# Strassen's seven products for the first layer of a second network, with its factors and input kept in a DRAM scratch

## The chip, the cores and the metric

The kernel runs on one NeuronCore of a Trainium2 chip. TensorE multiplies, VectorE (DVE), ScalarE (ACT) and GpSimd (POOL) do the elementwise work, SyncE (SP) issues every DMA. The metric is the device time of one execution in microseconds: the median of several runs.

## The reference

Three stages follow each other, all in float32:

```python
# attention, 4 batches x 8 heads x 576 positions x 64: local mask (4 heads), strided mask (4 heads)
scores = scale * q @ k.T, masked;  attn = softmax(scores);  x = attn @ v        # 2304 tokens x 512
# first network: maximum of three gates
h = np.maximum(np.maximum(x @ w1, x @ w2), x @ w3)                              # 512 -> 768
x = h @ w_out                                                                   # 768 -> 512
# second network: a leaky rectifier with a slope for each hidden unit
h = x @ w_in                                                                    # 512 -> 2048
g = np.maximum(h, 0.0) + alpha * np.minimum(h, 0.0)
out = g @ w_out                                                                 # 2048 -> 512
```

## The kernel before

Everything sits with features on the 128 partitions and tokens along the free axis. The networks' products are made in three passes: each operand is kept as two float32r words, `hi` (rounded by ScalarE) and `lo = a - hi` (subtracted by VectorE or GpSimd), and a product is hi*hi + hi*lo + lo*hi, three matmuls (`PAIRS`, L348). The helper `split` (L94) makes the two words, so all these operations carry the lines L96 and L99.

The weights arrive as 64-bit floats. `from_double` (L101) makes float32 of a block of 128 x 512: one ScalarE instruction (L112), two on VectorE (L115, L117), then the split (ScalarE, GpSimd). A `Converter` moves blocks through this line, one step per unit of TensorE's work.

The program is one order written out by hand. First come the four batches b = 0 to 3, each of 576 tokens. In a batch, 36 gate units (`gate_unit`, L354; 12 matmuls of 288 columns each) and 8 output units (`out1_unit`, L372; 18 matmuls each) of the first network are issued in turn. Between them stand the steps of the next batch's attention, and in batch 0 those of the weights' conversion. Batch 3 converts the second network's 32 blocks, and goes on with that in the first block of the second network. The result of the first network is copied from PSUM into x2 tiles that stay in SBUF (L380).

Then comes the second network over six blocks of 384 tokens. For each of 16 chunks f of 128 hidden units, `h_unit` (L493) issues 12 matmuls of 384 columns into one of three PSUM banks; VectorE applies the rectifier from PSUM (L502, L504), the split follows, and two chunks later `o_unit` (L512) adds the chunk into three output banks: 3 matmuls of 512 columns for each of 3 token tiles. After the 16th chunk each output bank is copied by ScalarE (L523) and stored (L524). All DMAs wait in SyncE's queue in program order.

Of the kernel before, what the change touches and what calls it, by code (L numbers as in the profile page):

```python
# [17 lines left out]
DM = 512  # L18
F1 = 768
F2 = 2048  # L20
P = 128
# [9 lines left out]
BLK = 384  # L31
NBLK = NT // BLK
BIG = -8.0e9
# [12 lines left out]
STARTS_LAST = tuple(range(1, NUNITS, 2))  # L46
LO_ON_POOL = (0, B - 1)
# [3 lines left out]
def attention_maxout_prelu_kernel(  # L51
# [49 lines left out]
    def from_double(raw, floats, dst, fetch):  # L101
# [19 lines left out]
        t = dst()  # L121
        split(t[:, 0], t[:, 1], a.bitcast(F32), nc.scalar, nc.gpsimd)
# [3 lines left out]
    hx, xx, x0x, ax, h0x, psx, stage_x = (ExitStack() for _ in range(7))  # L126
# [4 lines left out]
    wp = pool(ctx, "wp", 24)  # L131
    hp = pool(hx, "hp", 8)
    tp = pool(xx, "tp", 3)
# [187 lines left out]
    class Converter:  # L321


        def __init__(self, blocks, raws, floats):
            self.blocks, self.raws, self.floats = list(blocks), raws, floats
            self.sources = [src for src, _, _ in self.blocks]
            self.fetched, self.line = [], []
# [8 lines left out]
        def step(self):  # L336

            if self.blocks:
                _, key, weights = self.blocks.pop(0)

                def dst():
                    words[key] = weights().tile([P, 2, DM], F32R, tag="w", name="w")
                    return words[key]

                self.line.append(from_double(self.fetched.pop(0), self.floats, dst, self.fetch))
            self.line = [block for block in self.line if next(block, False)]
# [4 lines left out]
    x2 = {}  # L351
# [20 lines left out]
    def out1_unit(b, hf, dc, st):  # L372
        acc = bank()[:, :HALF]
        n = 0
        for f in range(NF1):
            for wi, xi in PAIRS:
# [3 lines left out]
        nc.scalar.copy(x2[b][:, dc, hf * HALF:(hf + 1) * HALF], acc)  # L380
# [5 lines left out]
    GATES = [(0, 0), (0, 1), (0, 2), (1, 0), (0, 3), (0, 4), (1, 1), (0, 5), None,  # L386
             (1, 2), (1, 3), (1, 4), (1, 5), None]
    GATES_LAST = [(hf, f) for f in range(NF1) for hf in range(2)] + [None, None]

    def first_net(b, gates, lo_engine, more):  # L390
        st = {}
        hf_out = 0
        for n, what in enumerate(gates):
# [5 lines left out]
            else:  # L399
                for g in range(3):  # L400
                    gate_unit(b, *what, g, st, lo_engine, hp if n < 8 else more)
                    yield


    x2h = {}

    def split_x2(x2p, blk):
        for cc in range(NCC):
            t = x2p.tile([P, 2, BLK], F32R, tag=f"x2h{cc}", name=f"x2h{cc}")
            done = 0  # L410
# [10 lines left out]
    blocks = [(w1[f, g], ("gate", f, g), lambda: wp) for f in range(NF1) for g in range(3)]  # L421
    blocks += [(wo1[f], ("mix", f), lambda: wp) for f in range(NF1)]
# [89 lines left out]
    def o_unit(blk, f, t):  # L512
# [6 lines left out]
        if f < NF2 - 1:  # L519
            return  # L520
# [87 lines left out]
```

## Time and profile before

| what | value |
|---|---|
| median of 3 runs | 815.6 us (815.19 to 816.21) |
| profiled execution, own time | 818.03 us |
| its span in the trace | 816.3 us |
| first network, batch 0 to batch 3 | to about 413 us of the span |
| second network | 413.0 to 812.6 us of the span |

The profile is read from the busy shares of the engines to the stretch in question, from there to the durations of single instructions, and last to the moments at which two engines want the same thing. A row of a group by line gives busy time, mean duration of one instruction and the idle time of the engine just ahead of it. A row of the timeline gives start, length and number of the instructions that were merged.

### The profile page before, as it was taken

Reading aid. Unit: us, or ns where it says so; the run is one execution under the profiler, and the core shown is the slowest. Engines: PE = TensorE matmul, PEld = TensorE weight load, DVE = VectorE, ACT = ScalarE, POOL = GpSimd, SP = SyncE. Lnnn points to the kernel's source line nnn. Section 1 sums busy time; section 2 is a strip of 40 time slices with the busy share of each in tenths; the row PEclk is TensorE's granted clock in tenths of the full one; section 3 lists DMA queues with packets and bytes.
Section 4 is the critical chain, followed back from the end, with each engine's and each line's share of the span. In section 5 each row is a group of like instructions: output and inputs, shape, how many; then the busy total and the mean of one; then the engine's idle time right before and its main releaser. Section 6 shows DMA issues by size and latency. Waiting matters only on the chain.

```text
span 816.3 us, 13289 instructions
## 1 busy us (share of the span) xinstructions
PE 789.7 (97%) x5200; PEld 735.2 (90%) x5200; DVE 378.5 (46%) x1006; ACT 281.0 (34%) x845; POOL 170.7 (21%) x176
## 2 busy tenths in 40 slices
PE   6688899999999999999999999999999999999998
PEld 5578799999999999999999999999999999999997
DVE  5669671243314423165657254454444445445442
ACT  7646683254324443255454121121111112112111
POOL 4456661022101111066458310000000000000000
PEclk9789899999999999999999999999999999999999
DMA  7437521020111100255444010001001001001001
GB/s 254 142 104 244 191 94 56 8 61 21 49 62 32 50 21 1 104 155 159 152 132 128 0 39 1 1 1 39 1 1 39 1 0 40 1 1 39 0 1 39
DMA packets 17775, 50.28 MB, mean 62 GB/s; under 512 B 2096, under 2 KB 2096, under 8 KB 17712
## 3 DMA queue, kind: packets, MB, share of 16 engines
q1 hardware_dynamic: 17712, 49.43, 18.6%
q8 instruction: 41, 0.67, 0.3%
q14 instruction: 22, 0.18, 0.1%
HBM read 44.70 MB, written 4.72 MB: 61 GB/s over the span
## 4 chain that ended last, share of the span: by engine, by line
PE 92%; ACT 3%; DMA 2%; DVE 2%; issue 1%; POOL 0%; SPq 0%; POOLq 0%; ACTq 0%; DVEq 0%
PE bank L359 27%; PE ph L498 25%; PE po L517 24%; PE bank L377 10%; PE bank L191 3%; PE bank L252 2%; PE bank L235 2%; ACT e L209 1%; DMA k<-in_kTs 1%; DMA raw<-in_w 1%; DVE word L115 1%; ACT word L112 0%; ACT w L96 0%; POOL e L223 0%; DVE e L203 0%
## 5 line engine op out<-in xcount | busy, mean ns | idle before, releaser
L359 PE MATMUL bank<-x,w 128*128 128x288 f32 x1728 | 247.3, 300 | 2.2 <-POOL w L99 2.2
L359 PEld LDWEIGHTS bank<-x,w 128*128 128x128 f32 x1728 | 232.6, 190 | 8.0 <-POOL w L99 2.4
L498 PE MATMUL ph<-x2h,w 128*128 128x384 f32 x1152 | 218.0, 339 | 0.0
L498 PEld LDWEIGHTS ph<-x2h,w 128*128 128x128 f32 x1152 | 205.4, 188 | 6.8
L517 PE MATMUL po<-w,g 128*128 128x512 f32 x864 | 210.2, 389 | 0.0
L517 PEld LDWEIGHTS po<-w,g 128*128 128x128 f32 x864 | 161.0, 188 | 26.7
L96 ACT CAST g<-neg 128x384 fp32r<-128x384 f32 x96 | 49.4, 514 | 315.8 <-DVE neg L504 315.8
L502 DVE TENSOR_SCALAR neg<-ph,alpha_sb 128x384 f32<-128x384 f32 x96 | 59.2, 617 | 155.1 <-PE ph L498 149.6
L366 DVE TENSOR_TENSOR t<-bank,t 128x288 f32<-128x288 f32 x96 | 43.7, 455 | 124.4 <-PE bank L359 111.8
L223 POOL TENSOR_TENSOR e<-e,rc 96x384 f32<-96x384 f32 (+2 forms) x64 | 49.1, 788 | 189.8 <-DVE rc L221 182.3
L99 POOL TENSOR_TENSOR w<-word,w 128x512 fp32r<-128x512 f32 x56 | 75.6, 1358 | 26.5 <-ACT w L96 24.2
L377 PE MATMUL bank<-h,w 128*128 128x288 f32 x576 | 80.3, 297 | 0.0
L209 ACT ACTIVATE e<-e,nm 96x128 f32<-96x128 f32 (+2 forms) x176 | 67.5, 386 | 32.6 <-DVE nm L203 32.6
L377 PEld LDWEIGHTS bank<-h,w 128*128 128x128 f32 x576 | 77.0, 188 | 1.3
L99 DVE TENSOR_TENSOR g<-neg,g 128x384 fp32r<-128x384 f32 x80 | 44.7, 559 | 52.4 <-ACT g L96 52.4
L117 DVE SCALAR_TENSOR_TENSOR word<-raw,word 128x512 uint32<-128x512 uint32 x56 | 54.8, 979 | 1.9
L504 DVE SCALAR_TENSOR_TENSOR neg<-ph,neg 128x384 f32<-128x384 f32 x96 | 53.5, 558 | 3.3
L96 ACT CAST h<-t 128x288 fp32r<-128x288 f32 x48 | 20.7, 432 | 83.8 <-DVE t L366 83.6
L115 DVE TENSOR_SCALAR word<-word 128x512 uint32<-128x512 uint32 x56 | 37.9, 677 | 8.4 <-ACT word L112 8.3
L191 PE MATMUL bank<-k,q 64*96 64x128 f32 (+2 forms) x352 | 30.0, 308 | 11.1 <-DMA k<-in_kTs 11.1
L112 ACT ACTIVATE word<-raw 128x512 f32<-128x512 f32 x56 | 37.5, 670 | 4.7 <-DMA raw<-in_w 4.3
L99 POOL TENSOR_TENSOR h<-t,h 128x288 fp32r<-128x288 f32 x24 | 25.8, 1076 | 62.0 <-ACT h L96 62.0
(39 smaller groups left out, 400.8 us busy)
## 6 DMA issues: line engine op xcount, KB each, us to landing
raw<-in_w SPq DMA_DIRECT2D x50, 512.0 KB, 3.6
q<-in_qT SPq DMA_DIRECT2D x16, 288.0 KB, 3.4
out_dram<-osb SPq DMA_DIRECT2D x18, 256.0 KB, 2.2
v<-in_vl SPq DMA_DIRECT2D x8, 384.0 KB, 3.0
raw<-in_wo SPq DMA_DIRECT2D x6, 512.0 KB, 3.6
v<-in_vs SPq DMA_DIRECT2D x8, 320.0 KB, 4.1
k<-in_kTl SPq DMA_DIRECT2D x8, 304.0 KB, 3.8
k<-in_kTs SPq DMA_DIRECT2D x8, 288.0 KB, 4.0
```

What stands on the lines that cost most here:

```text
L96: hi_engine.copy(hi, src)
L99: lo_engine.tensor_tensor(out=lo, in0=src, in1=hi.bitcast(F32), op=ALU.subtract)
L117: nc.vector.scalar_tensor_tensor(out=a, in0=low, scalar=29, in1=a, op0=ALU.logical_shift_right, op1=ALU.bitwise_or)
L191: nc.tensor.matmul(sc[j][:nq, KT * i:KT * i + nk], q[rows, qo:qo + nq], k[rows, ko:ko + nk], start=True, stop=True)
L209: nc.scalar.activation(e[:nq, j, i, :nk], e[:nq, j, i, :nk], AF.Exp, bias=nm[:nq, j, i:i + 1], scale=-1.0, accum_out=sm[:nq, j, i:i + 1])
L223: nc.gpsimd.tensor_tensor(out=e[:nq, j, :n, :nk], in0=e[:nq, j, :n, :nk], in1=rc[:nq, j, :n].unsqueeze(2).to_broadcast([nq, n, nk]), op=AL ...
L359: nc.tensor.matmul(acc, words["gate", f, g][:, wi, cc * P:(cc + 1) * P], xt[b, cc, hf][:, xi, :], start=n == 0, stop=n == 3 * NCC - 1)
L377: nc.tensor.matmul(acc, words["mix", f][:, wi, dc * P:(dc + 1) * P], st["h", hf, f][:, xi, :], start=n == 0, stop=n == 3 * NF1 - 1)
L498: nc.tensor.matmul(acc, words[0, f][:, wi, cc * P:(cc + 1) * P], x2h[blk, cc][:, xi, :], start=n == 0, stop=n == 3 * NCC - 1)
L502: nc.vector.tensor_scalar(out=neg, in0=acc, scalar1=0.0, scalar2=alpha_sb[:, f:f + 1], op0=ALU.min, op1=ALU.mult)
L504: nc.vector.scalar_tensor_tensor(out=neg, in0=acc, scalar=0.0, in1=neg, op0=ALU.max, op1=ALU.add)
L517: nc.tensor.matmul(acc, g[:, gi, t * P:(t + 1) * P], words[1, f][:, wi], start=f == 0 and i == 0, stop=f == NF2 - 1 and i == 2)
```

## The change

The second network now works on three blocks of 768 tokens, and on pairs of hidden chunks (`n` counts 24 groups: 8 pairs q for each of 3 blocks). The first layer of a pair is a 2 x 2 block product: two halves of the contraction, two chunks, two halves of 384 tokens. It is made with seven products in place of eight, of 6 matmuls each (2 contraction chunks x 3 passes), in two PSUM banks a and b_ that alternate (`h_products`). The sums of weights that this needs (`odd_chunk`) are made in batches 1 and 2, split, and stored to a DRAM scratch `hd`; in each group the four factors of the group after next are loaded from there (`load_pair`). The sums of x (`load_x2`) are made by GpSimd from the first network's result, which goes to DRAM in `out1_unit` and comes back. VectorE adds the products (`add`) and applies the rectifier from SBUF (`hidden`). The output products of group n (12 units of 3 matmuls, `o_units`) are issued between the products of group n+1.

Of the 16 second-layer chunks, 12 are converted in batch 3, and 4 in batch 2 by way of DRAM. In batch 3 the lo words of the first network are made by VectorE instead of GpSimd.

```diff
-BLK = 384
+BLK = 768
+HB = BLK // 2
+NQ = NF2 // 2
...
-LO_ON_POOL = (0, B - 1)
+DIRECT = 12
+CONVERT = tuple(15 * j // 4 for j in range(2 * NF2 - DIRECT))
+LOAD_X, SPLIT_X = 20, 35
...
+    def store(a, place):
+        t = wst.tile([P, 2, DM], F32R, tag="w", name="w")
+        n = a.shape[1]
+        nc.scalar.copy(t[:, 0, :n], a)
+        yield True
+        nc.vector.tensor_tensor(out=t[:, 1, :n], in0=a, in1=t[:, 0, :n].bitcast(F32), op=ALU.subtract)
+        yield True
+        nc.sync.dma_start(place[:, :, :n], t[:, :, :n].bitcast(F32))
...
+    def odd_chunk(q):
...
+            for out_, x, y, op in ((c[:, :half], e[:, :half], a[:, :half], ALU.subtract),
+                                   (a[:, :half], a[:, :half], a[:, half:], ALU.add),
+                                   (c[:, half:], a[:, :half], e[:, :half], ALU.subtract),
+                                   (d[:, :half], e[:, half:], c[:, half:], ALU.subtract)):
+                nc.vector.tensor_tensor(out=out_, in0=x, in1=y, op=op)
+            yield True
+            for x, place in ((a, hd[q][1]), (c, hd[q][2]), (d[:, :half], hd[q][3])):
+                yield from store(x, place)
...
     def out1_unit(b, hf, dc, st):
-        nc.scalar.copy(x2[b][:, dc, hf * HALF:(hf + 1) * HALF], acc)
+        xo = tp.tile([P, HALF], F32, tag="t", name="xo")
+        nc.scalar.copy(xo, acc)
...
+            nc.sync.dma_start(x2d[i][:, dc, s:s + nn], xo[:, done:done + nn])
...
+    def load_x2(blk):
+        for i in range(2):
+            t = xsp.tile([P, 2, 2, HB], F32, tag="xs", name="xs")
+            for h in range(2):
+                nc.sync.dma_start(t[:, :, h, :], x2d[2 * blk + h][:, i::2, :])
...
+            for out_, x, y in ((t3, b22, b12), (b12, b12, b11), (t2, b22, b12), (t4, b21, t2)):
+                nc.gpsimd.tensor_tensor(out=out_, in0=x, in1=y, op=ALU.subtract)
...
+    def split_x2(blk, k):
+        name = PRODUCTS[k][1]
+        for i in range(2):
...
+            split(t[:, 0], t[:, 1], xs.pop((blk, name, i)), nc.scalar, nc.gpsimd if blk else nc.vector)
...
-    gp = pool(ctx, "gp", 3)
-    ps_h = ctx.enter_context(tc.tile_pool(name="ps_h", bufs=3, space=PSUM, reuse_waits="tile"))
-    ps_o = ctx.enter_context(tc.tile_pool(name="ps_o", bufs=5, space=PSUM, reuse_waits="tile"))
+    gp = pool(ctx, "gp", 8)
+    cp = pool(ctx, "cp", 8)
+    osp = pool(ctx, "osp", 2)
+    ps_h = ctx.enter_context(tc.tile_pool(name="ps_h", bufs=2, space=PSUM, reuse_waits="tile"))
+    ps_o = ctx.enter_context(tc.tile_pool(name="ps_o", bufs=6, space=PSUM, reuse_waits="tile"))
...
+    def hidden(n, j, half, h):
+        f = 2 * (n % NQ) + j
+        neg = cp.tile([P, HB], F32, tag="c", name="neg")
+        nc.vector.tensor_scalar(out=neg, in0=h, scalar1=0.0, scalar2=alpha_sb[:, f:f + 1], op0=ALU.min, op1=ALU.mult)
+        nc.vector.scalar_tensor_tensor(out=neg, in0=h, scalar=0.0, in1=neg, op0=ALU.max, op1=ALU.add)
+        g = gts[n, j, half] = gp.tile([P, 2, HB], F32R, tag="g", name="g")
+        late.append(lambda: nc.scalar.copy(g[:, 0], neg))
+        if (j, half) != (0, 1):
+            late.pop()()
+        late.append(lambda: nc.vector.tensor_tensor(out=g[:, 1], in0=neg, in1=g[:, 0].bitcast(F32), op=ALU.subtract))
...
+        product(0, a)
+        u = temp()
+        nc.scalar.copy(u, a)
+        rest()
+        yield
+        product(1, b_)
+        v = temp()
+        add(v, b_, u)
+        yield
+        product(2, a)
+        add(u, a, u)
+        hidden(n, 0, 0, u)
+        yield
+        product(3, b_)
+        w = temp()
+        add(w, b_, v)
+        rest()
+        yield
+        product(4, a)
+        x = temp()
+        add(x, a, w)
+        add(v, a, v)
+        hidden(n, 1, 1, x)
+        yield
+        product(5, b_)
+        add(w, b_, w)
+        rest()
+        hidden(n, 1, 0, w)
+        yield
+        product(6, a)
+        add(v, a, v)
+        rest()
+        hidden(n, 0, 1, v)
+        yield
...
+    for n in range(NQ * NBLK):
+        blk, q = divmod(n, NQ)
+        if n + 2 < NQ * NBLK:
+            load_pair(n + 2)
+        if q == 4 and blk + 1 < NBLK:
+            load_x2(blk + 1)
+        for i, _ in enumerate(h_products(n)):
+            if n == 0 and EARLY_X + 1 + i < 7:
+                split_x2(0, EARLY_X + 1 + i)
+            elif q == NQ - 1 and blk + 1 < NBLK and i > 1:
+                split_x2(blk + 1, i - 2)
+            elif q == 0 and blk and i < 2:
+                split_x2(blk, 5 + i)
+            for _ in range((i + 1) * 12 // 7 - i * 12 // 7):
+                next(outs, None)
+        outs = o_units(n)
```

On TensorE, in the middle of the second network, this stood in a row before. A row is one line's matmuls: PSUM bank, x words, weight words, shape and count.

```order
L498 MATMUL ph_7568<-x2h0_7519,w_4344 128x384 x3
L498 MATMUL ph_7568<-x2h1_7522,w_4344 128x384 x3
L498 MATMUL ph_7568<-x2h2_7525,w_4344 128x384 x3
L498 MATMUL ph_7568<-x2h3_7528,w_4344 128x384 x3
L517 MATMUL po_7152<-w_5444,g_7516 128x512 x3
L517 MATMUL po_7156<-w_5444,g_7516 128x512 x3
L517 MATMUL po_7160<-w_5444,g_7516 128x512 x3
```

Now, from the sixth product of one group to the second of the next (x50 is the first half of the sixth product's x words, `ph_8060` bank a of one group, `ph_8184` the same bank in the next):

```order
L660 MATMUL ph_8061<-x50_7664,w_7800 128x384 x3
L660 MATMUL ph_8061<-x51_7667,w_7800 128x384 x3
L619 MATMUL po_7903<-w_4928,g_8007 128x512 x3
L619 MATMUL po_7882<-w_4890,g_8045 128x512 x3
L660 MATMUL ph_8060<-x60_7681,w_7804 128x384 x3
L660 MATMUL ph_8060<-x61_7684,w_7804 128x384 x3
L619 MATMUL po_7886<-w_4890,g_8045 128x512 x3
L619 MATMUL po_7903<-w_4890,g_8045 128x512 x3
L660 MATMUL ph_8184<-x00_7539,w_7928 128x384 x3
L660 MATMUL ph_8184<-x01_7542,w_7928 128x384 x3
L619 MATMUL po_7818<-w_4969,g_8099 128x512 x3
```

Twelve matmuls into one of three banks, then nine of the output, became six into one of two banks, then one or two output units of three.

On VectorE, where the second network begins, this stood before (word is a weight block under conversion, neg the rectified chunk):

```order
L117 SCALAR_TENSOR_TENSOR word_5030<-raw_4918,word_5030 128x512
L502 TENSOR_SCALAR neg_5110<-ph_5097,alpha_sb_64 128x384
L504 SCALAR_TENSOR_TENSOR neg_5110<-ph_5097,neg_5110 128x384
L115 TENSOR_SCALAR word_5079<-word_5079 128x512
L117 SCALAR_TENSOR_TENSOR word_5079<-raw_4979,word_5079 128x512
L502 TENSOR_SCALAR neg_5138<-ph_5125,alpha_sb_64 128x384
```

Now, from the last x words of the first block on (`ph_5552` is bank a, `ph_5553` bank b_, c the temporaries):

```order
L104 TENSOR_TENSOR x51_5565<-t_5028,x51_5565 128x384
L665 TENSOR_TENSOR c_5574<-ph_5553,c_5560 128x384
L104 TENSOR_TENSOR x60_5576<-xs_5013,x60_5576 128x384
L104 TENSOR_TENSOR x61_5579<-xs_5023,x61_5579 128x384
L665 TENSOR_TENSOR c_5560<-ph_5552,c_5560 128x384
L639 TENSOR_SCALAR neg_5589<-c_5560,alpha_sb_64 128x384
L641 SCALAR_TENSOR_TENSOR neg_5589<-c_5560,neg_5589 128x384
L665 TENSOR_TENSOR c_5600<-ph_5553,c_5574 128x384
L647 TENSOR_TENSOR g_5592<-neg_5589,g_5592 128x384
L665 TENSOR_TENSOR c_5609<-ph_5552,c_5600 128x384
L665 TENSOR_TENSOR c_5574<-ph_5552,c_5574 128x384
```

The x words and the additions of products stand in one queue, ahead of and between the reads that give the two banks back; the rectifier reads c in SBUF where it read ph in PSUM.

## Rows read from the trace of the kernel before

**Rows 1.** page, busy shares, and the granted clock in 40 slices

```profile
PE 789.7 (97%) x5200; PEld 735.2 (90%) x5200; DVE 378.5 (46%) x1006; ACT 281.0 (34%) x845; POOL 170.7 (21%) x176
...
PEclk9789899999999999999999999999999999999999
```

**Rows 2.** windows (PE, PEld, DVE, ACT, POOL busy): second network; batches 1-2; batch 3

```profile
413.00:812.60 399.60, 399.49 (x2018) 365.55 (x2016) 182.37 (x324) 80.41 (x167) 36.03 (x30) 1.00 0.07 23
148.00:337.50 189.50, 189.50 (x1596) 180.12 (x1595) 64.17 (x304) 76.47 (x296) 23.29 (x32) 1.00 0.13 40
337.50:412.00 74.50, 74.50 (x570) 74.50 (x569) 40.12 (x68) 35.00 (x75) 37.68 (x31) 1.00 0.46 142
```

**Rows 3.** timeline, TensorE in the second network: start us, us, engine, line, op

```profile
483.77 2.28 PE L498 MATMUL ph<-x2h,w 128*128 128x384 f32 x12
485.89 2.20 PE L517 MATMUL po<-w,g 128*128 128x512 f32 x9
487.93 2.28 PE L498 MATMUL ph<-x2h,w 128*128 128x384 f32 x12
```

**Rows 4.** groups by line and form: busy us, mean ns, idle before

```profile
L502 DVE TENSOR_SCALAR neg<-ph,alpha_sb 128x384 f32<-128x384 f32 x96 | 59.2, 617 | 155.1 <-PE ph L498 149.6 <-POOL g L99 5.5
...
L504 DVE SCALAR_TENSOR_TENSOR neg<-ph,neg 128x384 f32<-128x384 f32 x96 | 53.5, 558 | 3.3
L96 ACT CAST g<-neg 128x384 fp32r<-128x384 f32 x96 | 49.4, 514 | 315.8 <-DVE neg L504 315.8
L99 DVE TENSOR_TENSOR g<-neg,g 128x384 fp32r<-128x384 f32 x80 | 44.7, 559 | 52.4 <-ACT g L96 52.4
L366 DVE TENSOR_TENSOR t<-bank,t 128x288 f32<-128x288 f32 x96 | 43.7, 455 | 124.4 <-PE bank L359 111.8 <-ACT t L364 6.3 <-ACT word L112 3.2
...
L112 ACT ACTIVATE word<-raw 128x512 f32<-128x512 f32 x56 | 37.5, 670 | 4.7 <-DMA raw<-in_w 4.3 <-POOL w L99 0.3
```

**Rows 5.** source lines 115, 117, 366, 504, 99: duration ns min/median/max

```profile
L115 DVE TENSOR_SCALAR word<-word x56: 396/419/1811, 14.2 to 445.7; 128x512 uint32<-128x512 uint32 x56
...
L117 DVE SCALAR_TENSOR_TENSOR word<-raw,word x56: 691/693/2451, 15.2 to 446.2; 128x512 uint32<-128x512 uint32 x56
...
L366 DVE TENSOR_TENSOR t<-bank,t x96: 412/458/460, 42.2 to 394.2; 128x288 f32<-128x288 f32 x96
...
L504 DVE SCALAR_TENSOR_TENSOR neg<-ph,neg x96: 557/558/559, 416.0 to 807.1; 128x384 f32<-128x384 f32 x96
...
L99 POOL TENSOR_TENSOR g<-neg,g x16: 1017/1188/1319, 417.3 to 475.6; 128x384 fp32r<-128x384 f32 x16
```

**Rows 6.** timeline, VectorE and GpSimd at two moments

```profile
308.91 1.61 POOL L223 TENSOR_TENSOR e<-e,rc 96x384 f32<-96x384 f32 x2 [11.09 <-DVE rc L221]
...
310.19 0.64 DVE L99 TENSOR_TENSOR h<-t,h 128x288 fp32r<-128x288 f32 x1 [0.98 <-ACT h L96]
...
396.34 1.49 POOL L99 TENSOR_TENSOR w<-word,w 128x512 fp32r<-128x512 f32 x1
...
396.71 1.67 DVE L117 SCALAR_TENSOR_TENSOR word<-raw,word 128x512 uint32<-128x512 uint32 x1
```

**Rows 7.** timeline, TensorE in batch 0 beside two gaps

```profile
45.53 1.59 PE L359 MATMUL bank<-x,w 128*128 128x288 f32 x10 [2.19 <-POOL w L99]
48.58 1.52 PE L252 MATMUL bank<-pt,v 128*64 128x96 f32 x12 [1.47 <-ACT pt L238]
```

**Rows 8.** windows of the same place

```profile
44.00:48.00 4.00, 1.59 (x10) 1.36 (x10) 3.75 (x6) 1.57 (x4) 2.54 (x3) 1.00 0.23 33
48.00:52.00 4.00, 3.42 (x22) 3.18 (x23) 3.36 (x3) 3.11 (x8) 2.65 (x3) 0.51 0.62 229
```

**Rows 9.** timeline, the end of the program

```profile
810.42 3.10 SPq L524 DMA_DIRECT2D out_dram<-osb  x3
...
812.57 0.59 ACT L523 COPY osb<-po 128x512 f32<-128x512 f32 x1 [0.76 <-PE po L517]
```

**Rows 10.** DMA issues: KB each, median us to landing

```profile
out_dram<-osb SPq DMA_DIRECT2D x18, 256.0 KB, 2.2
```

More of the change, by code (lines that the diff above doesn't have):

```diff
@@ L485, in attention_maxout_prelu_kernel @@
     psx.close()
[L487 to L502 removed]
+    hw1 = pool(ctx, "hw1", 4)
@@ new lines, in attention_maxout_prelu_kernel, with o_unit @@
+    xmp1 = pool(ctx, "xmp1", 1)
+    gp = pool(ctx, "gp", 8)
[3 more added lines that the diff above has]
+    ps_o = ctx.enter_context(tc.tile_pool(name="ps_o", bufs=6, space=PSUM, reuse_waits="tile"))
+    gts, accs = {}, {}
+    def o_unit(n, j, t, first, last):
+        blk, q = divmod(n, NQ)
+        if q == 0 and first:
+            accs[blk, t] = ps_o.tile([P, DM], F32, tag="po", name="po")
+        acc = accs[blk, t]
+        g = gts[n, j, t // 3]
+        tt = t % 3
+        for i, (gi, wi) in enumerate(PAIRS):
+            nc.tensor.matmul(acc, g[:, gi, tt * P:(tt + 1) * P], words["o", 2 * q + j][:, wi],
+                             start=q == 0 and first and i == 0, stop=q == NQ - 1 and last and i == 2)
+        if q == NQ - 1 and last:
+            osb = osp.tile([P, DM], F32, tag="osb", name="osb")
+            rows = slice(blk * BLK + t * P, blk * BLK + (t + 1) * P)
+            nc.scalar.copy(osb, acc)
+            nc.sync.dma_start(out[rows, :], osb)
@@ L503, in h_unit, with o_units @@
+    def o_units(n):
+        for j, half, last in ((0, 0, False), (1, 0, True), (1, 1, False), (0, 1, True)):
+            for t in range(3 * half, 3 * half + 3):
+                yield o_unit(n, j, t, not last, last)
+    late = []
+    def hidden(n, j, half, h):
+        f = 2 * (n % NQ) + j
+        neg = cp.tile([P, HB], F32, tag="c", name="neg")
+        nc.vector.tensor_scalar(out=neg, in0=h, scalar1=0.0, scalar2=alpha_sb[:, f:f + 1],
                                 op0=ALU.min, op1=ALU.mult)
-        nc.vector.scalar_tensor_tensor(out=neg, in0=acc, scalar=0.0, in1=neg,
+        nc.vector.scalar_tensor_tensor(out=neg, in0=h, scalar=0.0, in1=neg,
@@ new lines, in hidden, with h_products, product, add @@
+        late.append(lambda: nc.scalar.copy(g[:, 0], neg))
+        if (j, half) != (0, 1):
+            late.pop()()
+        late.append(lambda: nc.vector.tensor_tensor(out=g[:, 1], in0=neg, in1=g[:, 0].bitcast(F32),
+                                                    op=ALU.subtract))
+    def h_products(n):
+        blk = n // NQ
+        banks = [ps_h.tile([P, HB], F32, tag="ph", name="ph") for _ in range(2)]
+        def product(k, bank):
+            (i, off), _ = PRODUCTS[k]
+            m = 0
+            for c in range(2):
+                for wi, xi in PAIRS:
+                    nc.tensor.matmul(bank, words["h", n, i][:, wi, off + c * P:off + (c + 1) * P],
+                                     x2h[blk, k, c][:, xi, :], start=m == 0, stop=m == 5)
+                    m += 1
+        def add(out_, bank, other):
+            nc.vector.tensor_tensor(out=out_, in0=bank, in1=other, op=ALU.add)
+        def rest():
+            while late:
+                late.pop(0)()
+        def temp():
+            return cp.tile([P, HB], F32, tag="c", name="c")
+        a, b_ = banks
+        product(0, a)
[32 more added lines that the diff above has]
+        yield
@@ L559 @@
+    while late:
+        late.pop(0)()
+    for _ in outs:
+        pass
 _SHAPES = ["in_qT", "in_kTl", "in_kTs", "in_vl", "in_vs", "in_w1", "in_wo1", "in_w2", "in_alpha"]
```

233 lines of the change are left out of this document (120 added, 113 removed).

## The prediction

> **What bounds the kernel now.** I read the page first: TensorE is busy for 97% of the span, and its granted clock is full (2.4 GHz) in nearly every slice but three near the start [rows 1]. So time is won only where TensorE has less to do, and lost where it is made to wait. The windows say where it never waits: 399.49 of 399.60 us in the second network, 189.50 of 189.50 in batches 1 and 2, 74.50 of 74.50 in batch 3 [rows 2]. The timeline gives the price of a matmul, from start to start: 12 of 384 columns take 485.89 - 483.77 = 2.12 us, 0.1767 each; 9 of 512 take 2.04 us, 0.2267 each [rows 3]. A chunk of one block costs 4.16 us, and 96 of them 399.4: the second network is exactly its matmuls. VectorE is busy for 182.4 of these 399.6 us, ScalarE for 80.4 [rows 2]; all that they do lies beside TensorE.
>
> **What the change removes.** Per pair of chunks and 768 tokens there were 48 matmuls of 384 columns, and there are now 7 x 6 = 42. Over 24 groups 144 go: 144 x 0.1767 = **-25.4 us**. The 864 of 512 columns stay. The smallest group is now 42 x 0.1767 + 36 x 0.2267 = 15.6 us (7.42 + 8.16).
>
> **What a steady group asks of VectorE.** Seven additions read PSUM: 455 ns for 288 elements [rows 4], some 555 for 384 (as L504, 558). Four times the rectifier and the lo word: L504's form 558, L99's 559 [rows 4], and the tensor_scalar, which now reads SBUF. The trace has no float32 one from SBUF; its bounds are 617 ns from PSUM [rows 4] and 419 ns for 512 uint32 elements from SBUF [rows 5]. I take 0.42, as the row with the same memory. Sum: 3.9 + 4 x 1.54 = 10.0 us of 15.6. The narrow place is the end of a group. Bank a comes back for the next group's first product only after the add behind product 6. Between the end of product 4 and that moment the queue holds add, add, two rectifier operations (2.1 us), then, from the end of product 5 on, add, lo word, two rectifier operations (2.1) and the add (0.56). TensorE takes 1.36 (two output units) + 1.06 (a product) for each step. VectorE ends the last add about 5.4 us after product 4, TensorE wants the bank after 6.2. It holds, with 0.8 us to spare. So steady groups cost 15.6 us, and nothing is added.
>
> **The first group (+5.7, and +1.5 for the clock).** Group 0 has no output units to lie between its products, so TensorE needs 7.42 us, and VectorE has, before it gives bank a back for group 1: six x lo words left over from the split (3.3 us at 0.56), seven adds (3.9), three rectifiers (2.9), two g lo words (1.1): 11.2 us. It can begin only 1.1 us in, since ScalarE first makes two x hi words (2 x 0.514, [rows 4]) in space that the first network's last matmuls free; with about half a microsecond of gaps that is 13. The cover is gone here: 13.1 - 7.4 = 5.7 (bounds 3 and 7). In batch 0, after gaps of 2.19 and 1.47 us [rows 7], the granted clock over the next 4 us was 0.51, the lower level of 1.2 GHz [rows 8]. Group 0 leaves gaps like these. At that rate 4 us lose 2; bounds 0 and 3, I take 1.5.
>
> **GpSimd beside VectorE (+5.4 and +3.0).** GpSimd was idle from the second block on. Now it makes 14 x lo words at each of two block changes, and 8 differences of x at n = 4 and n = 12: 44 instructions of at least 1.02 us [rows 5]. What this does to VectorE stands in two moments of the timeline. At 396.71 L117, with two SBUF inputs, takes 1.67 us instead of 0.69, ending when GpSimd's 396.34 + 1.49 = 397.83 has passed by 0.55; at 310.19 a lo word takes 0.64 instead of 0.46, beside a GpSimd pair that ends at 310.52 [rows 6]. Instructions with one input from PSUM never stretch: L366 has a maximum of 460 ns, L504 of 559 [rows 5]. Before, the rectifier read PSUM; now it reads SBUF, so that its two operations and the lo word, 12 per group, can all be held up, and only the adds can't. From the end of product 2 to the next group's first product TensorE needs 10.4 us, VectorE 6 adds (3.3) and 8 of the exposed operations (4.1): 3.0 us of slack. GpSimd puts 8 of its 14 subtractions there. If none meets, nothing is lost; if each of the 8 waits for a whole one, 8.2 - 3.0 = 5.2. Both engines alternate, and the lo words of x come behind ScalarE's copies, so I take five or six: 5.7 - 3.0 = 2.7 at each change, **+5.4**. The 8 differences fall wherever the x loads land, behind four factor loads; same bounds, 0 and 5.2 each, and part of them falls on slots with slack: 1.5 each, **+3.0**.
>
> The Trainium skill ("SBUF — State Buffer", section "Who interferes with whom") says that a VectorE instruction with two SBUF inputs, or in a two-port mode, and a GpSimd instruction that reads SBUF shut each other out for a whole instruction; the rows above agree, by 1.67 against 0.69. "VectorE: DVE Perf Modes", section "The perf-mode tier table", gives float32 tensor_scalar from SBUF the double rate, which is such a mode; no run here shows it. Without that mode it would be 0.2 us longer and never held up: the change of block would cost about 1.2 us in place of 2.7, and the sum -10.
>
> **Batches 1 and 2 (+1.5).** Twenty conversions move here: 20 x (0.42 + 0.69) [rows 5], 32 half-width sums at some 0.42, 28 lo words of 512 at about 0.69 (L99's 559 plus 128 elements) and 8 of 256: 22 + 13 + 23 = 58 us more on VectorE, from 64.2 to 122 of 189.5, or 65%. ScalarE gets 20 x 0.67 [rows 4] and 36 copies of about 0.6: 76.5 to 111, 58%. Batch 3 ran at 54% (40.12), 47% (35.00) and GpSimd at 51% beside a TensorE without gaps [rows 2]; this is somewhat more. Behind a late VectorE instruction stand the gates' maxima that give PSUM banks back; eight banks last for about four units. Stores and loads stand in one SyncE queue, and a ScalarE copy into a store's buffer waits for an earlier store (2.2 us for one of 256 KB, [rows 10]). Bounds 0 and 8; I take 1.5. Batch 3 gives up 20 of 32 conversions and takes 12 lo words: no change, its cover was whole and stays.
>
> **The end (+1.4).** The last three output banks finish within 1.4 us (two units of 0.68), and only two buffers take the copies. A copy takes 0.59 us [rows 9], its store lands 2.2 us after the issue [rows 10]: the first of the three is copied at -1.4 to -0.8, counted from the last matmul, and its buffer is free at 1.4, when the last copy can begin. It ends at 2.0 in place of 0.65. Loads of factors: 1.8 MB per group, two groups (31 us) ahead; hidden.
>
> **Sum.** -25.4 + 5.7 + 1.5 + 5.4 + 3.0 + 1.5 + 1.4 = -6.9. The profiled execution took 818.03 us itself, span 816.3; it would take 811.1. The median of the runs is 815.6, 2.4 lower than the profiled one; the same difference gives **808.7 us**.
>
> **Rivals.**
> A, GpSimd costs nothing: its 44 instructions fall between VectorE's, or into the 5.6 us that a group leaves free. Then -25.4 + 5.7 + 1.5 + 1.5 + 1.4 = -15.3: 800.3 us. For it: 10.0 of 15.6 us. Against it: the eight exposed operations stand close together.
> B, slower: GpSimd's lock at the block changes and the x differences, in VectorE's queue between the two banks. The other terms leave 15.3 us of gain; spread over 44 GpSimd instructions that is 0.35 us of each. If TensorE loses more than that for each, the kernel is slower; at half of 1.02, 44 x 0.51 = 22.4, and 22.4 - 15.3 = +7.1: 822.7. For it: the stretch of 1.67 us, and that each gap can bring the clock down. Against it: only 16 of the exposed operations lie in the narrow part of two groups.
> C, batches 1 and 2 begin to wait: the upper bound of 8 in place of 1.5 gives -0.4: 815.2. For it: 65%, in one queue with waits on DMA. Against it: batch 3's rows.
> That fewer matmuls are not issued is excluded by the order: six, then output units.
>
> **How the numbers follow.** Forecast 0.47, A 0.26, B 0.17, C 0.10. The forecast's own range is 803 to 814; with the other cases, 796 to 821. A difference below 0.2% (1.6 us) can't be told from none. Faster: nearly all of the forecast, A and a third of C, 0.75; same 0.06; slower B and the rest of C, 0.19.
>
> **What would show it.** In the profile after: 1008 matmuls of 384 columns at 0.177 us start to start; groups of 15.6 us; one gap of TensorE of about 5 us in pieces right behind the first network, released by VectorE's adds; gaps of 2 to 3 us in groups 7 and 15, beside stretched tensor_scalar and lo words; batches 1 to 3 without gaps. It is wrong if steady groups take more than 16 us, if a group of DMA loads comes late, or if batches 1 and 2 take more than 192 us.

## The result, and the profile after

The changed kernel takes 797.6 us (median of 4 runs, 796.39 to 798.86) beside 815.4 us for the kernel before. The ratio is 0.978 [0.976, 0.980], a gain of 17.8 us where 6.9 was forecast. The profiled execution took 798.86 us, with a span of 797.0; the one before took 818.03, so the traces differ by 19.2.

The page comes first, in the columns of [rows 1]. It is followed by windows in the columns of [rows 2]: the second network, batches 1 and 2, the stretch of batch 3, group 0, group 1, and a later group.

```profile
PE 770.7 (97%) x5056; PEld 709.8 (89%) x5056; DVE 499.5 (63%) x1264; ACT 303.6 (38%) x895; POOL 160.0 (20%) x168
...
L660 PE MATMUL ph<-x,w 128*128 128x384 f32 x1008 | 204.4, 338 | 2.5 <-ACT c L677 1.2
```

```profile
411.90:792.20 380.30, 377.67 (x1874) 338.11 (x1872) 247.75 (x462) 81.37 (x172) 49.48 (x44) 1.00 0.39 126
150.00:335.00 185.00, 184.57 (x1550) 174.98 (x1549) 118.15 (x411) 103.30 (x350) 28.52 (x32) 1.00 0.57 198
337.00:411.80 74.80, 74.80 (x568) 74.80 (x567) 42.36 (x80) 29.02 (x63) 9.46 (x8) 1.00 0.59 199
411.90:421.40 9.50, 8.35 (x44) 6.98 (x42) 8.04 (x17) 3.98 (x10) 0.00 (x0) 1.00 0.82 284
421.40:437.80 16.40, 16.27 (x81) 14.21 (x80) 12.19 (x26) 3.25 (x7) 0.00 (x0) 1.00 0.52 165
...
437.80:453.40 15.60, 15.60 (x79) 14.08 (x78) 9.34 (x20) 2.44 (x5) 0.00 (x0) 1.00 0.36 119
```

The second network went from 399.6 to 380.3 us. TensorE is idle for only 2.6 us of it, though VectorE is busy for 65% of it, GpSimd works in it, and the DMA engines carry 126 GB/s. The granted clock stayed full (2.4 GHz) in both first groups. Which waits are left is told by the view of TensorE's waits, which gives the waiting line, what it waited for, the total, the times and the longest:

```profile
PE ph L660 <- ACT c L677: 1.2, 2, 0.6
PE ph L660 <- DVE c L665: 0.5, 1, 0.5
PE ph L660 <- ACT g L644: 0.3, 1, 0.3
PE ph L660 <- issue: 0.3, 1, 0.3
```

None of them is a wait on a factor's load or on GpSimd. The same view of the weight loads, which go ahead of the matmuls, has four more that wait for VectorE's adds, 2.1 us in all. The starts of TensorE's runs of matmuls give the groups one by one. From group 2 on each takes 15.65 us (15.63 to 15.67), except for groups 9 and 17 with 16.5 (counted from 0; an expectation below calls them 8 and 16). From the first matmul of the network to the start of group 2 it is 25.88 us, where the matmuls need 7.42 + 15.64 = 23.06. From the last matmul at 792.0 to the end it is 5.0 us; before, it was 3.8.

Three moments explain most of this. The first is the step from group 0 to group 1, on VectorE and TensorE (timeline: start, length, instructions merged):

```profile
420.11 0.41 DVE L639 TENSOR_SCALAR neg<-c,alpha_sb 128x384 f32<-128x384 f32 x1
420.55 0.56 DVE L641 SCALAR_TENSOR_TENSOR neg<-c,neg 128x384 f32<-128x384 f32 x1
421.03 0.55 DVE L665 TENSOR_TENSOR c<-ph,c 128x384 f32<-128x384 f32 x1
...
423.14 0.55 DVE L665 TENSOR_TENSOR c<-ph,c 128x384 f32<-128x384 f32 x1
```

```profile
420.29 2.68 PE L660 MATMUL ph<-x,w 128*128 128x384 f32 x12 [0.27 <-issue]
422.81 0.86 PE L619 MATMUL po<-w,g 128*128 128x512 f32 x3
423.74 0.44 PE L660 MATMUL ph<-x,w 128*128 128x384 f32 x1
```

The 12 matmuls from 420.29 are product 6 of group 0 and product 0 of group 1 (six each). The add that reads product 6 runs from 423.14 to 423.69, and by then product 0 of the next group is done, so it went into the other bank. That bank had been read by the add at 421.03. The built program says the same of all 24 groups: products 0, 2, 4 and 6 are in bank 0 in the even groups and in bank 1 in the odd ones. So `ph_8060` and `ph_8184` of the order shown ahead, where they are called the same bank in two groups, are bank 1 and bank 0. Only product 1, at 423.74, comes right behind the add of 423.14. The same rows show VectorE's pace: 420.11, 420.55 and 421.03 are 0.44 and 0.48 us apart, while the second instruction is listed with 0.56. Instructions that follow each other without a wait overlap by about 0.1 us.

At the end of a steady group, here group 2, the adds behind products 5 and 6 are these:

```profile
449.81 0.56 DVE L665 TENSOR_TENSOR c<-ph,c 128x384 f32<-128x384 f32 x1 [0.49 <-PE ph L660]
...
452.24 0.56 DVE L665 TENSOR_TENSOR c<-ph,c 128x384 f32<-128x384 f32 x1 [0.48 <-PE ph L660]
```

Product 0 of group 3 starts at 453.42. The add behind product 6 ends 0.6 us before that, the add behind product 5, which gives it its bank, 3.1 us before.

The second moment is the end of group 7, where GpSimd makes the lo words of the next block's x:

```profile
524.30 1.25 DVE L647 TENSOR_TENSOR g<-neg,g 128x384 fp32r<-128x384 f32 x1
525.56 1.02 DVE L665 TENSOR_TENSOR c<-ph,c 128x384 f32<-128x384 f32 x2
526.50 1.12 DVE L639 TENSOR_SCALAR neg<-c,alpha_sb 128x384 f32<-128x384 f32 x1
527.65 1.25 DVE L641 SCALAR_TENSOR_TENSOR neg<-c,neg 128x384 f32<-128x384 f32 x1
...
530.02 1.21 DVE L639 TENSOR_SCALAR neg<-c,alpha_sb 128x384 f32<-128x384 f32 x1
531.26 1.25 DVE L641 SCALAR_TENSOR_TENSOR neg<-c,neg 128x384 f32<-128x384 f32 x1
532.44 0.55 DVE L665 TENSOR_TENSOR c<-ph,c 128x384 f32<-128x384 f32 x1
```

```profile
530.25 1.55 PE L619 MATMUL po<-w,g 128*128 128x512 f32 x6
531.64 1.20 PE L660 MATMUL ph<-x,w 128*128 128x384 f32 x6
```

Five instructions are stretched from 0.41 to 0.56 us to 1.12 to 1.25, about 0.7 each; the adds from PSUM are not. TensorE shows no gap, because the product that starts at 531.64 again doesn't wait for the add at 532.44, which ends 1.35 us after that start. In the whole network 36 instructions of VectorE are stretched by more than 0.08 us, by 19.9 us together. They lie in groups 4, 7, 8, 12, 15 and 16, and each of these groups takes 15.63 to 15.67 us.

The third moment is the gap of group 9, on ScalarE and then TensorE:

```profile
551.23 0.59 ACT L624 COPY osb<-po 128x512 f32<-128x512 f32 x1 [3.22 <-DMA out_dram<-osb]
551.71 0.48 ACT L677 COPY c<-ph 128x384 f32<-128x384 f32 x1
```

```profile
552.25 1.31 PE L660 MATMUL ph<-x,w 128*128 128x384 f32 x6 [0.64 <-ACT c L677]
```

The copy of an output bank waits for the store of an earlier one. Behind it in ScalarE's queue stands the copy of a group's first product, and TensorE waits for the bank which that copy frees.

### The profile page after: what moved, and what is told of

Read it like the earlier page. It is cut to its first block, busy times and chain, and to the rows that moved or that the text cites. A ratio compares the mean times of both kernels' runs of the same rounds, so it can differ in the third digit from the quotient of the medians.

```text
span 797.0 us, 13816 instructions
## 1 busy us (share of the span) xinstructions
PE 770.7 (97%) x5056; PEld 709.8 (89%) x5056; DVE 499.5 (63%) x1264; ACT 303.6 (38%) x895; POOL 160.0 (20%) x168
## 4 chain that ended last, share of the span: by engine, by line
PE 88%; ACT 3%; DMA 3%; DVE 3%; issue 1%; SPq 1%; POOL 0%; ACTq 0%; POOLq 0%; DVEq 0%
PE bank L418 26%; PE po L619 24%; PE ph L660 21%; PE bank L436 10%; PE bank L201 3%; PE bank L262 2%; PE bank L245 2%; DMA k<-in_kTs 1%; DMA out_dram<-osb 1%; ACT e L219 1%; DVE word L120 1%; DMA q<-in_qT 1%; ACT word L117 0%; ACT osb L624 0%; DVE e L213 0%
## 5 line engine op out<-in xcount | busy, mean ns | idle before, releaser
L619 PE MATMUL po<-w,g 128*128 128x512 f32 x864 | 224.8, 392 | 0.0
L660 PE MATMUL ph<-x,w 128*128 128x384 f32 x1008 | 204.4, 338 | 2.5 <-ACT c L677 1.2
L660 PEld LDWEIGHTS ph<-x,w 128*128 128x128 f32 x1008 | 180.3, 188 | 18.6 <-DVE c L665 2.1
L665 DVE TENSOR_TENSOR c<-ph,c 128x384 f32<-128x384 f32 x168 | 91.2, 554 | 82.6 <-PE ph L660 82.2
L233 POOL TENSOR_TENSOR e<-e,rc 96x384 f32<-96x384 f32 (+2 forms) x64 | 54.3, 868 | 184.2 <-DVE rc L231 159.3
L647 DVE TENSOR_TENSOR g<-neg,g 128x384 fp32r<-128x384 f32 x96 | 55.3, 576 | 38.0 <-ACT g L644 37.2
L641 DVE SCALAR_TENSOR_TENSOR neg<-c,neg 128x384 f32<-128x384 f32 x96 | 62.0, 646 | 3.3
L489 POOL TENSOR_TENSOR t<-xs 128x384 f32<-128x384 f32 x12 | 13.4, 1115 | 206.4 <-DMA xs<-x 205.9
L639 DVE TENSOR_SCALAR neg<-c,alpha_sb 128x384 f32<-128x384 f32 x96 | 49.2, 512 | 0.9
L120 DVE TENSOR_SCALAR word<-word 128x512 uint32<-128x512 uint32 x56 | 32.0, 571 | 12.5 <-ACT word L117 12.3
```

Of the source, the lines that this page charges most:

```text
L233: nc.gpsimd.tensor_tensor(out=e[:nq, j, :n, :nk], in0=e[:nq, j, :n, :nk], in1=rc[:nq, j, :n].unsqueeze(2).to_broadcast([nq, n, nk]), op=AL ...
L619: nc.tensor.matmul(acc, g[:, gi, tt * P:(tt + 1) * P], words["o", 2 * q + j][:, wi], start=q == 0 and first and i == 0, stop=q == NQ - 1 a ...
L641: nc.vector.scalar_tensor_tensor(out=neg, in0=h, scalar=0.0, in1=neg, op0=ALU.max, op1=ALU.add)
L647: late.append(lambda: nc.vector.tensor_tensor(out=g[:, 1], in0=neg, in1=g[:, 0].bitcast(F32), op=ALU.subtract))
L660: nc.tensor.matmul(bank, words["h", n, i][:, wi, off + c * P:off + (c + 1) * P], x2h[blk, k, c][:, xi, :], start=m == 0, stop=m == 5)
L665: nc.vector.tensor_tensor(out=out_, in0=bank, in1=other, op=ALU.add)
```

## The experiments

All ratios are to the kernel before, which was measured beside each of the twelve. The edits shown are to the changed kernel.

### An eighth product

```diff
         product(0, a)
+        product(0, a)
```

The first product is computed twice, with the same result. Expected:

> Each group makes its first product twice into the same bank (the second overwrites the first), so 48 matmuls of 384 columns per group again, with the whole new structure of loads, adds and lo words around them. Theory 1 (the removed matmuls pay in full, 0.1767 us each, and nothing else of the change costs much): groups of 16.71 us instead of 15.65, the kernel 24 x 1.06 = 25.4 us above the changed one, about 823 us, that is 7 to 8 us slower than before. Rival (part of the gain is something else than the matmuls, for instance a different pace of the rest): clearly less than 25, for instance 15 to 20 us.

Measured: 821.8 us, ratio 1.009 [1.005, 1.012], so 24.2 us above the changed kernel. One group of it, and its second network:

```profile
439.00:455.70 16.70, 16.70 (x85) 15.16 (x84) 9.39 (x20) 2.43 (x5) 0.00 (x0) 1.00 0.36 111
411.52:814.30 402.78, 401.67 (x2018) 363.30 (x2016) 244.83 (x462) 81.55 (x171) 49.45 (x44) 1.00 0.37 119
```

A group grows from 15.65 to 16.68, by 1.03 where six matmuls at 0.1767 are 1.06. The gaps at the block changes are gone, presumably because one product more gives ScalarE time. So the term of the matmuls is confirmed (25.4 was expected), and the rest of the new structure costs only some 6.5 us (821.8 - 815.3) when it buys nothing.

### Each name on its own bank

```diff
-    ps_h = ctx.enter_context(tc.tile_pool(name="ps_h", bufs=2, space=PSUM, reuse_waits="tile"))
+    ps_a, ps_b = (ctx.enter_context(tc.tile_pool(name=name, bufs=1, space=PSUM, reuse_waits="tile"))
+                  for name in ("ps_a", "ps_b"))
...
-        banks = [ps_h.tile([P, HB], F32, tag="ph", name="ph") for _ in range(2)]
+        banks = [p.tile([P, HB], F32, tag="ph", name="ph") for p in (ps_a, ps_b)]
```

This is the kernel that the forecast worked out: seven products alternate, so that products 6 and 0 use the same bank. Expected:

> The two PSUM banks of the products get a pool each, so that the first product of every group goes to bank a, which the last product of the group before has just used; in the changed kernel the trace suggests that it goes to the other one, b_. Theory 1 (the room at a group's end comes from this): steady groups stay at 15.65 us; group 0 grows from 9.5 to about 11.6, since group 1 waits for the add behind product 6 (at 423.7 instead of 421.6 us); in groups 7 and 15, where GpSimd holds VectorE up, gaps of 1 to 2.5 us before the next group's first product; together +3 to +7 us. Rival (the bank doesn't matter, VectorE is early enough anyway): 0, group 0 at 9.5 us.

Measured: 804.9 us, ratio 0.987 [0.984, 0.990], 7.2 above the changed kernel. The last add of group 0, and the product behind it:

```profile
422.36 0.55 DVE L666 TENSOR_TENSOR c<-ph,c 128x384 f32<-128x384 f32 x1
```

```profile
422.96 2.29 PE L661 MATMUL ph<-x,w 128*128 128x384 f32 x6 [2.16 <-DVE c L666]
```

```profile
PE ph L661 <- ACT g L645: 2.8, 3, 1.3
PE ph L661 <- DVE c L666: 2.7, 2, 2.2
PE ph L661 <- ACT c L678: 1.7, 2, 0.9
PE ph L661 <- issue: 0.3, 1, 0.3
```

The wait that the forecast described is now there, and it is gone in the changed kernel because there the bank changes from group to group. The clock falls behind it as well. Over the next 3.44 us the granted clock is 0.52, which is 1.2 GHz for nearly all of the time and loses some 1.65 us:

```profile
422.96:426.40 3.44, 3.44 (x10) 3.17 (x11) 1.64 (x4) 0.96 (x3) 0.00 (x0) 0.52 0.17 55
```

Groups 0 and 1 take 29.11 us (+6.05 over their matmuls, where the forecast had 5.7 + 1.5). The three groups at each block change are together 2.6 us over 3 x 15.65: 1.5 in groups 7 and 8 (15 and 16), where GpSimd works, and 1.1 in group 9 (17), behind the output copy. The two groups with x differences are 0.36 over. Steady groups are unchanged at 15.65.

### Four output buffers

```diff
-    osp = pool(ctx, "osp", 2)
+    osp = pool(ctx, "osp", 4)
```

Expected:

> Four buffers for the output copies instead of two. Theory: the gaps of 0.5 to 0.6 us behind the block changes (ScalarE's copy of the first product stands behind an output copy that waits for its buffer's store) go, and the last copy starts right behind the last matmul: groups 8 and 16 from 16.5 to 15.65 us, the end from 4.8 to 3.8 us behind the last matmul; -2.5 us in all, about 795. Rival (the stores themselves set the end, the gaps come from elsewhere): less than 0.5 us.

Measured: 796.5 us, ratio 0.976 [0.973, 0.979]. In its trace all groups from 2 on take 15.65, and the end is 3.66 us in place of 5.02: the two terms, 1.7 and 1.4, are the buffers'. The medians differ by only 1.1, where 2.5 was expected, and they were not measured side by side; that comparison is made again below.

### The first block's last x words on GpSimd

```diff
-                  nc.gpsimd if blk else nc.vector)
+                  nc.gpsimd if blk or k >= EARLY_X else nc.vector)
```

Six subtractions of group 0 go from VectorE to GpSimd. Expected:

> The six x lo words that stand in VectorE's queue in group 0 (products 4 to 6 of the first block) go to GpSimd. Theory (VectorE's queue is what makes group 0 take 9.5 us instead of 7.4): group 0 takes 8.3 to 8.8 us, -1 us in all. Rival (GpSimd's 1.02 us each, and its lock, are worse than VectorE's 0.47): group 0 as long or longer, 0 to +1.5 us, with TensorE waiting for a GpSimd lo word.

Measured: 799.95 us, ratio 0.980 [0.976, 0.984]. Groups 0 and 1 take 25.44 in place of 25.88: a gain of 0.4 in place of 1. Gaps of 0.86, released by ScalarE's g, and 0.41 take the place of the three smaller ones. The total says nothing at this size, since the first network of its profile ended 2.4 us later.

### GpSimd made busy in every group

```diff
+    def extra(n, i, count):
+        key = ((n - 1, 1, 0), (n - 1, 0, 1), (n - 1, 0, 1), (n, 0, 0), (n, 0, 0), (n, 1, 1), (n, 1, 0))[i]
+        for _ in range(count if key in gts else 0):
+            y = dp.tile([P, HB], F32, tag="y", name="y")
+            g0 = gts[key][:, 0].bitcast(F32)
+            nc.gpsimd.tensor_tensor(out=y, in0=g0, in1=g0, op=ALU.subtract)
...
+            extra(n, i, 1)
```

Seven subtractions per group whose results nobody reads. Expected:

> The changed kernel with seven more GpSimd subtractions in each of the 24 groups (384 elements, two SBUF inputs, about 1.02 us, read from the g words of the same or the last group, so that they are spread over the group; their result is used by nothing). 168 in all, against the 44 of the change. Theory 1 (VectorE is held up, but has room: it works about 9 us of 15.65 and each GpSimd instruction costs it about 0.46 us): VectorE's three SBUF instructions stretch to 0.5 to 0.7 us in the mean, groups stay at 15.65 us outside the block changes, the kernel 0 to +2 us against 797.6. Rival (the forecast: 0.19 us of TensorE for each GpSimd instruction): +32 us, groups of 17 us. Second rival (GpSimd does not hold VectorE at all): durations as without, 0.

Measured: 805.4 us, ratio 0.988 [0.985, 0.991], 7.8 above the changed kernel. Its profiled run took 801.5, and in that the second network is 4.7 longer; the other four runs are about 4 us slower than the profiled one (805.07 to 806.26), and no trace tells why. Steady groups stay at 15.65. What grows is the two block changes (groups 8 and 9 take 16.57 + 17.25, groups 16 and 17 16.58 + 17.55) and groups 0 and 1 (26.9). In groups 9 and 17 it is again the wait for ScalarE's copy, now of 1.4 and 1.6 us. The expected 0 to 2 was too low, and the first rival's 32 is refuted. So is the second rival, that GpSimd doesn't hold VectorE at all: VectorE's busy time in steady groups goes from 9.4 to some 11 us.

With `extra(n, i, 2)`, fourteen per group, GpSimd is nearly full. Expected:

> Fourteen more GpSimd subtractions in each group, 14.3 us of GpSimd in 15.65. Theory 1: VectorE needs about 8.9 + 14 x 0.46 = 15.3 us of each group and is at its limit; the groups begin to grow, to 16 to 17.5 us, the kernel +8 to +45 us: the room is used up, and TensorE waits for VectorE's adds. Rival (no lock): still 15.65.

Measured: 820.9 us, ratio 1.006 [1.004, 1.009]. Two steady groups in the windows, then minimum, median and maximum of the rectifier's two operations (ns), then TensorE's waits:

```profile
440.60:456.27 15.67, 15.67 (x80) 14.12 (x78) 13.19 (x20) 2.31 (x6) 13.87 (x15) 1.00 0.38 118
456.27:471.90 15.63, 15.63 (x79) 14.11 (x78) 13.62 (x19) 2.46 (x5) 13.46 (x14) 1.00 0.39 118
```

```profile
L647 DVE TENSOR_SCALAR neg<-c,alpha_sb x96: 408/980/1190, 418.0 to 807.1; 128x384 f32<-128x384 f32 x96
```

```profile
L649 DVE SCALAR_TENSOR_TENSOR neg<-c,neg x96: 559/1065/1264, 418.4 to 808.2; 128x384 f32<-128x384 f32 x96
```

```profile
PE ph L668 <- POOL x L104: 9.3, 15, 1.4
PE ph L668 <- DVE c L673: 3.3, 5, 1.2
PE ph L668 <- ACT g L652: 2.5, 3, 1.1
```

The lock is there with full force: the tensor_scalar's median goes from 0.415 to 0.98 us, the other's from 0.559 to 1.065. VectorE's busy time per group goes from 9.4 to 13.4 us, that is 4.0 for 14 instructions, 0.29 each. And TensorE still shows no gap in these groups. The total lies in the expected range, but not by the growth of every group that was expected. Of the 23 us, 19 are lost at the block changes (groups 7 to 9 take 16.35 + 24.4 + 16.4, groups 15 to 17 16.4 + 24.45 + 16.5), mostly because x's lo words are late on a full GpSimd.

The seven on GpSimd again, with the fixed banks. Expected:

> Seven more GpSimd subtractions in each group, and the two product banks fixed, so that each group's first product waits for the add behind the last product of the group before. Theory 1 (with this bank order the slack at a group's end is below 1 us, as the forecast had it): each group shows a gap of 0.5 to 1.5 us before its first product, groups of 16.2 to 17.2 us, +12 to +35 us above the run with fixed banks alone (804.9). Rival (the bank order is not what gives the room): as with seven and free banks, that is +0 to +2 above 804.9.

Measured: 810.4 us, ratio 0.993 [0.991, 0.996], 5.5 above the kernel with fixed banks. My expectation of 12 to 35 failed: even with product 0 behind the add, steady groups mostly stay at 15.65. The reason is not a larger slack at that place. In these groups the add behind product 6 ends 0.63 us before the next product 0, the same as without the seven and near the 0.8 of the forecast. VectorE, which in the changed kernel idles for 0.5 us before that add, has caught up with TensorE by then. In groups 4, 8, 12 and 16, where GpSimd's other work comes on top, it hasn't, and they take 16.4 to 16.7.

### VectorE made busy in every group

The same `extra` with `nc.vector.tensor_tensor`: seven subtractions of 384 elements per group on VectorE, GpSimd as in the changed kernel. Expected:

> The changed kernel with seven more VectorE subtractions per group (384 elements, both inputs from a g word; one per product; their result is used by nothing), to measure the room in VectorE's queue directly. Theory 1 (VectorE's instructions follow each other every 0.47 us, a group has 19 of them, 8.9 us, and 6.7 us of room): groups stay at 15.65 us outside the block changes, +0 to +3 us. Rival (the forecast's count: 10.0 us per group and only 0.8 us of slack in the last three products): about +0.9 us per group, +20 us.

Measured: 811.9 us, ratio 0.995 [0.993, 0.996], 12.5 above the changed kernel, measured beside it. The expected 0 to 3 was too low, because the block changes grew; for the other groups it held: steady groups stay at 15.65, those with x differences grow by 0.3 and 0.7, and the two block changes by 5.7 and 5.6. A block change in its windows:

```profile
540.00:545.00 5.00, 2.96 (x15) 2.33 (x14) 5.00 (x6) 2.17 (x5) 5.00 (x5) 1.00 0.00 0
545.00:550.00 5.00, 5.00 (x19) 4.57 (x20) 4.93 (x9) 1.48 (x3) 2.53 (x3) 0.66 0.02 8
```

Here both engines work without a break, TensorE waits for 2.04 us, and behind that wait its granted clock falls to 0.66 over 5 us, a mix of 1.2 and 2.4 GHz. The block change's waits of 0.76, 2.04 and 0.63 us and 5 x 0.34 = 1.7 us of lower clock make 5.1 of the 5.7. This is the mechanism that the forecast saw, lock and clock, at a load which the changed kernel doesn't have.

Fourteen on VectorE. Expected:

> Fourteen more VectorE subtractions per group: 8.9 + 14 x 0.47 = 15.5 us of 15.65. Theory 1: at the edge; groups of 15.65 to 16.5 us, with gaps before a product that waits for VectorE, +5 to +25 us. Rival (durations of 0.56 count, 10.0 + 7.8 = 17.8 us per group): groups of 17.8 us or more, +52 us.

Measured: 830.9 us, ratio 1.018 [1.014, 1.022], 31.5 above the changed kernel where 5 to 25 was expected. One steady group, and VectorE's own rows in it:

```profile
441.02:456.69 15.67, 15.67 (x79) 14.12 (x78) 15.50 (x35) 2.62 (x6) 0.00 (x0) 1.00 0.40 119
```

```profile
441.92 0.55 DVE L673 TENSOR_TENSOR c<-ph,c 128x384 f32<-128x384 f32 x1
442.39 0.55 DVE L655 TENSOR_TENSOR g<-neg,g 128x384 fp32r<-128x384 f32 x1
442.86 0.41 DVE L647 TENSOR_SCALAR neg<-c,alpha_sb 128x384 f32<-128x384 f32 x1
443.31 0.56 DVE L649 SCALAR_TENSOR_TENSOR neg<-c,neg 128x384 f32<-128x384 f32 x1
443.78 1.02 DVE L616 TENSOR_TENSOR y<-g 128x384 f32<-128x384 f32 x2
```

VectorE is busy for 15.50 of 15.67 us and the group still takes 15.65. Its 33 instructions by their durations are 10.0 + 14 x 0.555 = 17.8 us, which would not fit. They follow each other every 0.45 to 0.47 us, and 33 x 0.47 = 15.5 does. The pace, not the duration, is what an instruction costs. The rival's groups of 17.8 are refuted. The loss is again where GpSimd works: 25.0 and 25.8 us in groups 8 and 16, 18.6 in groups 4 and 12 with the x differences.

### Both edits that promised something

Four output buffers, and the first block's x words on GpSimd. Expected:

> Four output buffers, and the first block's last six x lo words on GpSimd. Theory: the sum of the two, -1.7 us (block changes), -1.4 us (end), -0.4 us (group 0): 794 us, ratio to before 0.974. Rival (one of them gives back what the other won): 796 to 798.

Measured: 795.5 us, ratio 0.975 [0.973, 0.978], between the two expectations. A window in which the changed kernel has its gap of group 9, and here none:

```profile
545.00:552.00 7.00, 7.00 (x37) 6.38 (x36) 3.44 (x7) 2.97 (x6) 0.00 (x0) 1.00 0.52 173
```

The changed kernel and this one were then run again beside each other. Expected of the changed kernel:

> The changed kernel as it is, beside the others on one chip. All theories: 797 to 799 us, ratio 0.978; its first network may end anywhere between 410 and 414 us of the span, as in the runs so far.

and of the other:

> Four output buffers and the first block's late x lo words on GpSimd, beside the changed kernel. Theory: 2 to 3.5 us faster than the changed kernel in the same call (1.7 at the block changes, 1.4 at the end, 0.4 in group 0). Rival: within 1 us of it.

Measured: 799.4 us (796.78 to 801.27), ratio 0.979 [0.975, 0.983], and 796.25 us (793.34 to 796.90), ratio 0.975 [0.972, 0.978]. That is 3.1 us; the traces account for 1.7 at the block changes (1.4 in the repeat), 1.4 at the end and 0.4 in groups 0 and 1. The two intervals overlap, so the size is not settled by the times alone; that the gaps are gone is shown by both traces, where every group from 2 on takes 15.65. It has the lowest medians here; four output buffers alone, at 796.5, are not told apart from it.

## Why the prediction was right in direction and wrong in size

**The matmuls (-25.4): right.** 1008 of them stand in the page, steady groups take 15.65 where 15.6 was forecast, and the eighth product costs 24.2.

**The first group (+7.2 forecast, 2.8 measured): its size failed, in the step "Bank a comes back for the next group's first product only after the add behind product 6".** The program's names a and b_ are not the two banks: with seven products and one pool of two, the next group's first product went to the bank that had come free earlier. With the banks fixed by name, groups 0 and 1 cost 6.05, near the forecast. The clock's share of 1.5 was nothing in the changed kernel, where gaps of 0.54, 0.28 and 0.27 us left it at 1.00; with fixed banks it came, with some 1.65. So the reasoning nearly held for the bank that it assumed, and the assumption was wrong. Most of the 2.8 that is left is time in which group 0 and the start of group 1 wait for VectorE's adds.

**GpSimd beside VectorE (+5.4 and +3.0 forecast, 0 measured): failed.** The held instructions exist, five of them at the end of group 7, about as many as the forecast counted. Wrong was what they are set against. First the bank, as above: the forecast's 0.8 us of slack was about right for the add behind product 6 (0.6), but the add that counts is the one behind product 5, with 3.1 us. At the end of group 7 the two are -1.35 and 2.3. In the kernel with fixed banks a block change costs 1.5 and not 2.7, the x differences 0.36 each time and not 1.5. So the bank accounts for 3.7 of the 8.4 us; the other 4.7 were not there even with the forecast's bank. For these there are two more reasons, and no run tells how they divide. Second the price: a held instruction lost 0.7 us (3.6 for the five), not the 1.02 of a whole one. Third VectorE's load, 10.0 us per group by durations: at a pace of 0.47 it is 19 x 0.47 = 8.9, which leaves 6.7 us of room and not 5.6. The trace before had this already. Four lo words of 384 elements are merged there into one row, in the timeline of VectorE at the end of the first network:

```profile
402.15 1.97 DVE L99 TENSOR_TENSOR x2h<-x,x2h 128x384 fp32r<-128x384 f32 x4 [3.77 <-ACT x2h L96]
```

By the 559 ns of [rows 4] they would take 2.24. In steady groups of the changed kernel the room takes either load alone, 14 more on VectorE or 14 on GpSimd. The other bank has a part in that: with 14 on VectorE the add behind product 6 ends 1.45 us after the next product 0 has started (441.92 + 0.55, beside 441.02), with 14 on GpSimd 0.1 to 2.1 us after it in groups 1 to 6, so fixed banks would presumably not have carried either load. TensorE waits where both loads come together, or where a full GpSimd is late with x's words. The Trainium skill ("SBUF — State Buffer", section "Who interferes with whom") has it that the later of the two engines is shut out for the whole instruction. The trace agrees that they exclude each other (0.415 to 1.23 us at most), but on average over the steady groups with fourteen extra subtractions one of them (median 0.94 us) cost VectorE 0.29 us of busy time, and TensorE nothing.

**What the forecast left out (+1.7).** Two output buffers were counted at the end, but the same wait stands at both block changes, since ScalarE's queue puts the copy of a product behind the copy of an output bank. Four buffers remove it.

**Batches 1 and 2 (+1.5) and the end (+1.4): about right**, with 0.4 us of idle time in 185 (0 to 1.2 in the other profiles) and 1.2.

**The sum.** -25.4 + 2.8 + 1.7 + 0.4 + 1.2, and 22 x 0.06 = 1.3 for steady groups that are a little over 15.59, give -18.0. The profiles differ by 19.2. The rest is within what the first network's end moves by: 409.9 to 414.3 us between the profiles of kernels that have the same first network, with different waits on k's loads and on GpSimd's e in batch 0. Why these vary stays open, and so does why four runs of the kernel with seven subtractions on GpSimd took 4 us more than its profiled one. Rival A, in which GpSimd costs nothing, was the case that came true, and it was still 2.7 us too high, mostly by the first group.

## What to carry to other kernels

Load an engine by the distance from start to start of instructions that follow each other, not by the listed duration; here that is 15% less and decides whether there is room. A name in the program is not a buffer: before pricing a wait on a bank, find out which earlier tile's reader gave that bank back. And look at each small pool wherever it is used, since a wait on an output buffer stops everything that stands behind it in that engine's queue, here a product's bank.

## What was not expected of the hardware

- VectorE's float32 instructions of 384 elements last 0.55 to 0.56 us, but start every 0.47 (tensor_scalar from SBUF: 0.41 and 0.45); 33 of them fit into 15.65 us.
- The float32 tensor_scalar from SBUF takes 0.415 us for 384 elements, 0.617 from PSUM [rows 4]. "VectorE: DVE Perf Modes" of the Trainium skill, section "The perf-mode tier table", gives the first the double rate, and the trace agrees.
- GpSimd at 13.5 of 15.65 us stretches three of VectorE's four operations, the median of the tensor_scalar from 0.415 to 0.98 us, and the steady groups lose nothing by it.
- The granted clock stayed at 1.00 behind single gaps of up to 1.6 us (seven subtractions on GpSimd). It fell to 1.2 GHz behind waits of 2.04 us (seven on VectorE) and 2.16 us (fixed banks), and with fourteen on GpSimd behind 0.78, 0.49 and 1.35 us within 5 us.
